# Moving three on-chip transposes of a recurrent attention kernel from TensorE to the DMA engines

## The chip, the cores and the metric

The kernel runs on one core of one Trainium2 chip. The metric is the device time of one execution in microseconds (us). The before and changed kernels were run in turn on the same chip. "PE" is TensorE, "PEld" its weight loads, "DVE" VectorE, "ACT" ScalarE, "POOL" GpSimd and "SP" the engine that issues the DMAs here.

## The reference, cut to what matters

Two identical layers follow each other. Each has an attention part A that walks over 64 segments of 32 rows and hands 8 memory rows from one segment to the next, and a gated feed-forward part B. Every part starts with a norm of its rows.

```
x = x + _A_ref(_layernorm(x), A_mem0, Wq, Wk, Wv, Wo, 32)   # layer 0
x = x + _B_ref(_layernorm(x), W_gate, W_up, W_down)
x = x + _A_ref(_layernorm(x), A_mem0, Wq, Wk, Wv, Wo, 32)   # layer 1, the same weights
x = x + _B_ref(_layernorm(x), W_gate, W_up, W_down)
# in _A_ref, for each segment s:
    h = concatenate([mem, xs])             # 8 + 32 rows of 448
    scores = q @ k^T / 16, masked;  p = softmax(scores);  o = (p @ v) @ Wo
    mem = o[:, :8];  outs.append(o[:, 8:])
```

## The kernel before: the parts that matter

The kernel runs layer 0 on segment t and layer 1 on segment t-4 in one step, 68 steps in all, two steps to a "pair" p of segments. Within a step the instructions go roughly: products of the keys with the folded query-key weights (hT,Mw, 224 matmuls), scores (TTm, TTs), softmax, P transposed (PTs), P @ h (PTs,hK), and for the memory rows the shorter chain PTm,hK, then Nw,UTm, then hi and lo, then selm,hi, whose result goes into the hT of the next step. Once a pair, the rest of the output projection (un), the norm of its rows (ln_b), the feed-forward part (b_layer) and the norm for the pair two later (ln_a).

Three blocks have to be transposed, because the products that read them take them with rows and columns exchanged: the rows of ln_a (xn into hT), the rows of ln_b (xn into xBT) and the probabilities (Ps into PTs). All three go through TensorE and are then copied out of PSUM:

```python
def ln_transpose(self, i, wr):
    T = S.tile("R", 1)
    S.mm(lambda: [MM(T.b().bitcast(BF)[:, c*128:c*128+128], S.xn[:, i, c*128:c*128+128], S.ident[:, :], is_transpose=True)
                  for c in range(4)], 4 * S.pitch(128), [("xn", i, 0), ("xn", i, 1), ("ident",)], T.res() + wr)
    return T
def ln_a(self, p):
    S.ln(S.XA[:, p % 4, :], ...)                       # row statistics, xn
    T = S.ln_transpose(0, [("hTx", pp, s) for s in range(2)])
    for s in range(2):
        S.cp(lambda s=s: S.hT[:, pp, s, :, :, 0:SEG], lambda s=s: ..., 256, T.res(), [("hTx", pp, s)])   # PSUM -> SBUF
    ...
def ln_b(self, p):                                     # the same, into xBT with one copy
def seg_pt(self, t):                                   # the same from Ps, into PTs with one copy
```

The order of instructions is not written by hand. The kernel lists operations with an estimated duration for each engine, and a list scheduler in it (class `_Order`) walks through a model of the engines and picks, at each free moment, the ready operation with the highest priority. A table `BIAS` adds a constant to the priority of each kind of operation.

## Time and profile before

| | before |
|---|---|
| time, median (range) of 4 runs | 1663.48 us (1662.29 to 1666.5) |
| span of the profiled run, granted PE clock | 1662.0 us, 0.994 |
| PE busy / idle | 1614.9 / 47.1 us |
| DVE, ACT busy | 1141.2, 717.2 us |

Idle is the span less the busy time. The first line of the page says the same; each entry is busy us, share of the span and number of instructions:

```profile
PE 1614.9 (97%) x30742; PEld 1192.9 (72%) x30742; DVE 1141.2 (69%) x3172; ACT 717.2 (43%) x2051; POOL 93.3 (6%) x156
```

PE is what bounds: it is busy for 97% of the span, and its groups show hardly any waiting. These are groups of PE instructions, each shape apart: line, operation, output and operands, shapes, count, then busy us and mean ns of one, then the idle time of PE just before the group and what ended it:

```profile
L127 PE MATMUL b<-hT,Mw 128*128 128x80 bf16 x13440 | 496.0, 202 | 0.7 <-ACT hT L696 0.7
L127 PE MATMUL b<-xBT,big 128*128 128x128 bf16 x3248 | 195.5, 219 | 0.4 <-DVE lo L913 0.4
L127 PE MATMUL b<-Nw,UTm 128*32 128x448 bf16 x3752 | 193.1, 357 | 2.1 <-DVE UTm L697 1.0 <-ACT UTm L696 0.6
L127 PE MATMUL b<-ident,xn 128*128 128x128 bf16 x276 | 27.7, 224 | 11.1 <-DVE xn L733 7.0 <-DVE seln L569 4.1
L127 PE MATMUL b<-ident,Ps 128*128 128x128 bf16 x272 | 26.7, 220 | 1.7 <-DVE Ps L859 1.7
L127 PE MATMUL b<-selm,hi 128*128 128x16 bf16 x268 | 22.0, 171 | 3.4 <-DVE lo L913 1.5
L127 PE MATMUL b<-PTs,hK 40*64 40x256 bf16 x256 | 20.6, 292 | 1.8 <-ACT big L696 0.5
```

The groups ident,xn and ident,Ps are the transposes. The busy time of these overlapping matmuls, 54.4 us, is not what they hold PE for: from start to next start, the two groups hold 40.2 us between 100 and 1655 us.

How close the hT hand-over is to its user can be read only from the timeline. This is the before kernel at the start of a pair; columns are start us, length us, engine, what, and in brackets the idle before it:

```profile
843.42 0.61 DVE L733 TENSOR_SCALAR xn<-XA,stat 128x448 bf16<-128x448 bf16 x2
844.08 0.40 PE L127 MATMUL b<-ident,xn 128*128 128x128 bf16 x4 [0.23 <-DVE xn L733]
844.52 0.49 DVE L697 COPY hT<-b 128x256 bf16<-128x256 bf16 x2 [0.49 <-PE b L127]
...
846.96 0.57 PE L127 MATMUL b<-Nw,big 128*64 128x448 bf16 x4
...
847.51 0.27 PE L127 MATMUL b<-hT,Mw 128*128 128x80 bf16 x3
```

The norm is done at 844.03, hT is complete at 845.01, and the segment that reads it starts at 847.51. So the hand-over took 1.0 us and had 2.5 us to spare. From the end of the norm to the start of its segment it is 3.48 us here and 4.98 us in the pairs between.

### The profile page before, as it was taken

The numbers are of one execution on the slowest core, as the hardware profiler recorded it, in microseconds if no ns is written. First come the engines' busy times: TensorE is split into PE (matmuls) and PEld (weight loads), VectorE is DVE, ScalarE is ACT, GpSimd is POOL, SyncE is SP. The second block draws the span as 40 slices with busy tenths as digits, with TensorE's granted clock in tenths as the row PEclk, the third lists the DMA queues.
The fourth block names the chain that finished last, engine by engine and source line by source line (L and its number), as shares of the span: only waits on it lengthen the run. The fifth ranks groups of instructions, "written<-read, shape, count | busy, mean of one in ns | idle before, by whom it ended". The sixth has DMA issues, their size and how long they took to land. (4 is left out here: it accounts for less than half of the span.)

```text
span 1662.0 us, 68199 instructions
## 1 busy us (share of the span) xinstructions
PE 1614.9 (97%) x30742; PEld 1192.9 (72%) x30742; DVE 1141.2 (69%) x3172; ACT 717.2 (43%) x2051; POOL 93.3 (6%) x156
## 2 busy tenths in 40 slices
PE   5999999999999999999999999999999999999998
PEld 2567777777776777777777777777677777766775
DVE  8757767666767767676776766676676767676665
ACT  4623443445343444544343444434334453433442
POOL 4000000000000000000000000000000000000000
PEclk8999999999999999999999999999999999999999
DMA  9710000000000000000000000000000000000000
GB/s 234 207 40 5 4 3 6 6 5 5 5 5 6 5 4 6 6 4 6 6 5 4 5 5 5 4 6 6 5 6 5 5 6 4 5 3 4 4 4 6
DMA packets 55762, 27.54 MB, mean 17 GB/s; under 512 B 44584, under 2 KB 54576, under 8 KB 55472
## 3 DMA queue, kind: packets, MB, share of 16 engines
q1 hardware_dynamic: 55120, 22.94, 5.7%
q8 instruction: 242, 3.96, 1.0%
q14 instruction: 48, 0.39, 0.1%
q10 hardware_dynamic: 352, 0.24, 0.1%
HBM read 10.33 MB, written 1.84 MB: 7 GB/s over the span
## 5 line engine op out<-in xcount | busy, mean ns | idle before, releaser
L127 PEld LDWEIGHTS b<-hT,Mw 128*128 128x128 bf16 x15232 | 535.2, 100 | 16.9 <-issue 8.6
L127 PE MATMUL b<-hT,Mw 128*128 128x80 bf16 (+1 forms) x15232 | 544.0, 199 | 3.2 <-issue 1.8
L127 PE MATMUL b<-Nw,big 128*64 128x448 bf16 (+1 forms) x1936 | 307.8, 355 | 0.6 <-DVE big L697 0.5
L697 DVE CAST TTs<-b 128x320 bf16<-128x320 f32 (+5 forms) x542 | 244.8, 454 | 13.2 <-PE b L127 12.5
L127 PE MATMUL b<-xBT,big 128*128 128x128 bf16 (+1 forms) x3920 | 217.1, 214 | 0.4 <-DVE lo L913 0.4
L127 PEld LDWEIGHTS b<-xBT,big 128*128 128x128 bf16 x3920 | 203.2, 98 | 7.2 <-ACT UTm L696 4.8
L127 PEld LDWEIGHTS b<-Nw,big 128*64 128x64 bf16 (+1 forms) x1936 | 128.8, 104 | 105.7 <-issue 14.0
L127 PE MATMUL b<-Nw,UTm 128*32 128x448 bf16 x3752 | 193.1, 357 | 2.1 <-DVE UTm L697 1.0
L696 ACT ACTIVATE TTm<-b 64x64 bf16<-64x64 f32 (+5 forms) x338 | 76.7, 227 | 266.7 <-PE b L127 262.7
L1053 DVE TENSOR_TENSOR hB<-gT,b 128x256 bf16<-128x256 bf16 x227 | 91.1, 412 | 119.4 <-ACT gT L1052 108.2
L127 PEld LDWEIGHTS b<-Nw,UTm 128*32 128x32 bf16 x3752 | 100.8, 97 | 88.7 <-issue 15.7
L697 POOL COPY hK<-xn 32x448 bf16<-32x448 bf16 x136 | 75.9, 558 | 1466.9 <-DVE xn L733 1460.4
L696 ACT ACTIVATE TTs<-b 64x256 bf16<-64x256 f32 (+4 forms) x342 | 141.4, 413 | 30.3 <-PE b L127 24.2
L697 DVE CAST TTm<-b 128x80 bf16<-128x80 f32 (+5 forms) x546 | 126.0, 233 | 38.9 <-PE b L127 10.2
L696 ACT ACTIVATE big<-b 128x512 bf16<-128x512 f32 (+1 forms) x242 | 124.5, 555 | 30.7 <-PE b L127 29.9
L697 DVE CAST UTm<-b 128x448 bf16<-128x448 f32 (+2 forms) x124 | 80.2, 647 | 81.0 <-PE b L127 80.1
L1052 ACT ACTIVATE gT<-b 128x256 bf16<-128x256 f32 x227 | 85.6, 380 | 90.7 <-PE b L127 73.0
L697 DVE CAST big<-b 128x512 bf16<-128x512 f32 (+1 forms) x146 | 85.4, 596 | 25.0 <-PE b L127 22.6
L127 PE MATMUL b<-big,hB 128*128 128x448 bf16 (+1 forms) x490 | 98.8, 354 | 0.0
L912 ACT ACTIVATE hi<-b 128x448 bf16<-128x448 f32 x67 | 36.5, 544 | 121.4 <-PE b L127 119.8
L127 PE MATMUL b<-PTs,hK 40*128 40x512 bf16 (+1 forms) x640 | 83.6, 346 | 4.8 <-ACT PTs L696 1.5
L696 ACT ACTIVATE UTm<-b 128x448 bf16<-128x448 f32 (+2 forms) x127 | 64.6, 523 | 24.4 <-PE b L127 23.3
(105 smaller groups left out, 1503.3 us busy)
## 6 DMA issues: line engine op xcount, KB each, us to landing
big<-in_A_Wo_dram SPq DMA_DIRECT2D x3, 896.0 KB, 5.8
out_dram<-ys SPq DMA_DIRECT2D x32, 56.0 KB, 1.9
big<-in_B_W_down_dram SPq DMA_DIRECT2D x1, 1568.0 KB, 7.1
XA<-in_A_x_dram SPq DMA_DIRECT2D x28, 56.0 KB, 2.2
big<-in_B_W_up_dram SPq DMA_DIRECT2D x1, 1344.0 KB, 5.9
big<-in_B_W_gate_dram SPq DMA_DIRECT2D x1, 1344.0 KB, 8.8
Nw<-in_A_Wo_dram SPq DMA_DIRECT2D x1, 896.0 KB, 6.4
XA<-in_A_x_dram ACTq DMA_DIRECT2D x4, 56.0 KB, 4.3
```

What stands on the lines that cost most here:

```text
L127: ins = E.matmul(out, lhsT=lhsT, rhs=rhs, **kw)
L696: return E.activation(out(), src(), ACT.Copy)
L697: return E.tensor_copy(out(), src())
L912: S.act(lambda E: E.activation(S.hi[:, :], C.b()[:, 0:D], ACT.Copy), D, C.res(), [("hi",)])
L1052: S.act(lambda E, k=k, R=R, n=n: E.activation(S.gT[:, k % 2, 0:n], R[0].b()[:, 0:n], ACT.Relu), n, R[0].res(), [("gT", k % 2)])
L1053: S.dve(lambda E, k=k, R=R, n=n, fcs=fcs: E.tensor_tensor(S.hB[:, fcs[0]:fcs[-1] + 1, 0:w], S.gT[:, k % 2, 0:n].rearrange("p (a b) -> p a ...
```

## The change

The intent: TensorE bounds, SP and the DMA engines are nearly idle after the weights are loaded (from 100 us on, the issues held SP for 28.7 us, and the DMA share was 0.02), so let the DMA engines transpose. The change gives each ln_a four transposes of 32x512, because the hT layout keeps 8 memory keys beside every 32 rows; its rows grow from 40 to 48 elements in it. The priorities were tuned anew.

```diff
+KROW = 48
 BIAS = {
-    "b_down": -5000.0, "b_layer": 2000.0, "ln_a": 41619.0, "p_t_mem": 500.0, "s_mem": 74990.0, ...
+    "b_down": -8324.0, "b_layer": -10663.0, "ln_a": -45000.0, "ln_b": 45000.0, "m_nat": -6708.0, ...
-        self.hT = self.sb("hT", [128, 2, 2, 4, 2, KEYS])
+        self.hT = self.sb("hT", [128, 2, 2, 4, 2, KROW])
     def ln_a(self, p):
-        T = S.ln_transpose(0, [("hTx", pp, s) for s in range(2)])
         for s in range(2):
-            S.cp(lambda s=s: S.hT[:, pp, s, :, :, 0:SEG], ..., 256, T.res(), [("hTx", pp, s)])
+            for l in range(2):
+                a = 64 * l + 32 * s
+                S.tdma(f"hT{s}{l}", lambda s=s, l=l: S.hT[:, pp, s, :, l, 0:SEG], lambda a=a: S.xn[a:a + 32, 0, :], 32,
+                       [("xn", 0, 0), ("xn", 0, 1)], [("hTx", pp, s, l)])
     def ln_b(self, p):
-        T = S.ln_transpose(1, [("xBT",)])
-        S.cp(lambda: S.xBT[:, :, :]..., 512, T.res(), [("xBT",)])
+        S.tdma("xBT", lambda: S.xBT[:, :, :], lambda: S.xn[:, 1, :], 128, [("xn", 1, 0), ("xn", 1, 1)], [("xBT",)])
+    def tdma(self, name, out, src, rows, rd, wr):
+        self.q.add("dma", ("sp",), {"sp": 60.0 + 4.0 * rows}, lambda E: E.dma_start_transpose(out=out(), in_=src()), rd, wr, name=name)
     def seg_pt(self, t):
-        (four transposes of Ps on TensorE and a copy of 512 columns)
+        S.tdma("pts", lambda: S.PTs[...], lambda: S.Ps[...], 128, [("Ps",)], [("PTs",)])
... (the readers of hT take 40 of its 48 elements; unchanged otherwise)
```

More of the change, by code (lines that the diff above doesn't have):

```diff
@@ L152 @@
 BIAS = {
-    "b_down": -5000.0, "b_layer": 2000.0, "ln_a": 41619.0, "p_t_mem": 500.0, "s_mem": 74990.0, "s_seg": 72560.0,
-    "seg_pt": -859.0, "u_mem": -38520.0, "u_seg": 2000.0, "un": -37811.0,
+    "b_down": -8324.0, "b_layer": -10663.0, "ln_a": -45000.0, "ln_b": 45000.0, "m_nat": -6708.0, "m_t": -3095.0,
+    "p_t_mem": 39621.0, "s_mem": 30914.0, "s_seg": 4852.0, "seg_pt": -500.0, "u_mem": -34712.0, "u_seg": -25197.0,
+    "un": -36918.0,
 }
@@ L289, in run @@
                 lim = max(f, t0) + (60.0 if e == "pe" else 40.0)
-                t, o = max((x for x in lst if x[0] <= lim), key=lambda x: (x[1].prio, -x[0]))
+                stay = BIAS.get("stay", 0.0) if e == "pe" else 0.0
+                t, o = max((x for x in lst if x[0] <= lim), key=lambda x: (x[1].prio + stay * (x[1].mode == mode), -x[0]))
                 if best is None or (t, -o.prio) < (best[0], -best[2].prio):
@@ L735, in ln @@
                   b - a, rd + [(key, 1), (key, 2)], [("xn", i, n)], 2)
-    def ln_transpose(self, i, wr):
-        S = self
-        T = S.tile("R", 1)
-        S.mm(lambda: [MM(T.b().bitcast(BF)[:, c * 128:c * 128 + 128], S.xn[:, i, c * 128:c * 128 + 128], S.ident[:, :], is_transpose=True)
-                      for c in range(4)], 4 * S.pitch(128), [("xn", i, 0), ("xn", i, 1), ("ident",)], T.res() + wr)
-        return T
     def ln_a(self, p):
@@ L747, in ln_a @@
         S.ln(S.XA[:, p % 4, :], [("XA", p % 4, 0), ("XA", p % 4, 1)], 0, "lnA", 0)
-        T = S.ln_transpose(0, [("hTx", pp, s) for s in range(2)])
         for s in range(2):
-            S.cp(lambda s=s: S.hT[:, pp, s, :, :, 0:SEG],
-                 lambda s=s: T.b().bitcast(BF)[:, 0:512].rearrange("p (c l s q) -> p c l s q", c=4, l=2, s=2)[:, :, :, s, :],
-                 256, T.res(), [("hTx", pp, s)])
+            for l in range(2):
+                a = 64 * l + 32 * s
+                S.tdma(f"hT{s}{l}", lambda s=s, l=l: S.hT[:, pp, s, :, l, 0:SEG], lambda a=a: S.xn[a:a + 32, 0, :], 32,
+                       [("xn", 0, 0), ("xn", 0, 1)], [("hTx", pp, s, l)])
         for s in range(2):
@@ L761, in ln_b @@
         S.ln(S.XB[:, p % 2, :], [("XB", p % 2, i) for i in range(3)], 16, "lnB", 1)
-        T = S.ln_transpose(1, [("xBT",)])
-        S.cp(lambda: S.xBT[:, :, :].rearrange("p a b -> p (a b)"), lambda: T.b().bitcast(BF)[:, 0:512], 512, T.res(), [("xBT",)])
+        S.tdma("xBT", lambda: S.xBT[:, :, :], lambda: S.xn[:, 1, :], 128, [("xn", 1, 0), ("xn", 1, 1)], [("xBT",)])
+    def tdma(self, name, out, src, rows, rd, wr):
+        self.q.add("dma", ("sp",), {"sp": 60.0 + 4.0 * rows}, lambda E: E.dma_start_transpose(out=out(), in_=src()), rd, wr, name=name)
     def t_unit(self, t, c, u0, m):
@@ L777, in mms @@
             return [MM(b[:, j * n:j * n + n], S.M[:, kt, 16 * c + u0 + j, :],
-                       S.hT[:, pp, s, kt, l0:l1, :].rearrange("p l x -> p (l x)"), start=(kt == 0), stop=(kt == 3))
+                       S.hT[:, pp, s, kt, l0:l1, 0:KEYS], start=(kt == 0), stop=(kt == 3))
                     for j in range(m) for kt in range(4)]
-        rd = [("hTx", pp, s)] + S.mkeys(pp, s, l0, l1)
+        rd = [("hTx", pp, s, l) for l in range(l0, l1)] + S.mkeys(pp, s, l0, l1)
         if t == 0:
@@ L806, in s_mem @@
         C = S.tile("R", 1)
-        S.mm(lambda: [MM(C.b()[:, l * KEYS:l * KEYS + KEYS], S.TTm[:, c, l, :], S.hT[:, pp, s, c, l, :], start=(c == 3), stop=(c == 2))
+        S.mm(lambda: [MM(C.b()[:, l * KEYS:l * KEYS + KEYS], S.TTm[:, c, l, :], S.hT[:, pp, s, c, l, 0:KEYS], start=(c == 3), stop=(c == 2))
                       for l in range(l0, l1) for c in (3, 0, 1, 2)], 100.0 * nl,
-             [("TTm",) + k for k in S.TKEYS] + [("hTx", pp, s)] + S.mkeys(pp, s, l0, l1), C.res())
+             [("TTm",) + k for k in S.TKEYS] + [("hTx", pp, s, l) for l in range(l0, l1)] + S.mkeys(pp, s, l0, l1), C.res())
         st = S.stat
@@ L835, in mms @@
                         out.append(MM(b[:, (qd * 2 + l) * KEYS:(qd * 2 + l) * KEYS + KEYS],
-                                      S.TTs[:, c, l, qd * 4:qd * 4 + 4, :].rearrange("p u q -> p (u q)"), S.hT[:, pp, s, c, l, :],
+                                      S.TTs[:, c, l, qd * 4:qd * 4 + 4, :].rearrange("p u q -> p (u q)"), S.hT[:, pp, s, c, l, 0:KEYS],
                                       start=False, stop=(l == l1 - 1 and qd == 3 and c == 2)))
@@ L862, in seg_pt @@
         S = self
-        G = S.tile("R", 1)
-        S.mm(lambda: [MM(G.b().bitcast(BF)[:, a * 128:a * 128 + 128], S.Ps[:, a, :], S.ident[:, :], is_transpose=True) for a in range(4)],
-             4 * S.pitch(128), [("Ps",), ("ident",)], G.res() + [("gseq",), ("PTs",)])
-        S.cp(lambda: S.PTs[:, :], lambda: G.b().bitcast(BF)[:, 0:512], 512, G.res(), [("PTs",)])
+        S.tdma("pts", lambda: S.PTs[:, :].rearrange("p (a x) -> p a x", a=4), lambda: S.Ps[:, :, :].rearrange("p a x -> p (a x)"), 128,
+               [("Ps",)], [("PTs",)])
     def p_t_mem(self, t):
```

## The prediction

> **What bounds it.** TensorE. The windows view has PE busy 1534.5 of the 1555 us from 100 to 1655, at clock 1.00; VectorE is busy 1063.8 and ScalarE 669.8 there. In the waits view the longest rows are other engines waiting for PE. So time goes out with PE start-to-start time and comes back with new PE waits.
>
> **What is removed.** 276 + 272 TensorE transposes (xn and Ps, by-form groups) in 137 groups of four. In the timeline of 800 to 893 us a group holds PE 0.22 us, or 0.33 us where it stands between products of another tiling (a switch costs about 0.10 us). From 100 to 1655 us that sums to 40.2 us; some switches stay, so I count 34 us. Also removed: the evictions PTs (597 ns x68), xBT (597 ns x35), hT (286 ns x62, some on ScalarE): about 80 us of engines that don't bound. The new order has about 7 fewer tiling switches per four segments.
>
> **What is added.** Per segment one 128x512 SBUF transpose by DMA for the probabilities, per pair four 32x512 and one 128x512 for the norms. Estimate of their latency from the weight transposes of this trace: 1024x448 holds the SP queue 3.7 us and lands about 2.2 us later; scaled by bytes a 128x512 takes 0.55 + 2.2 = 2.8 us, a 32x512 2.4 us. [...] no SBUF-to-SBUF transpose is in this trace. TensorE plus eviction took about 1.1 us, so each hand-over gets some 1.7 us longer. hT rows go from 40 to 48 elements, so the 80-column operand is in two pieces; I expect no cost, but 1 ns on each of 13440 matmuls would be 13 us.
>
> **On the critical path?** From the last scores to Ps took 2.9 to 3.2 us, so PTs is ready about 5.9 us after the scores. In the new order the PE work before the first product with PTs is, by measured starts, about 6.9, 9.4, 7.7 and 6.9 us in the four segments of a period: hidden, 1 to 3 us to spare. hT has two segments of slack: hidden. xBT after the odd-even product is the tight one: norm chain 3.5 to 4.1 us + 2.8 against about 6.1 us of work, so 0.5 to 1 us of wait, and the UTm product there has no filler after PTm, about 0.8 us. So per period (93.5 us) about 2.5 us out and 1.2 us back. Start: first hT and PTs transposes queue behind weight loads, +2 us. End: two bare norm transposes, +3 us.
>
> **Predicted:** 1640 us (-1.4%), 8 in 10 within 1620 to 1662. Faster over 2%: 0.27; within 2%: 0.63; slower: 0.10.
>
> **What would show it.** No ident,xn and ident,Ps groups; PE matmul count lower by 548; issue-to-landing of PTs and xBT 2.5 to 3.2 us in the DMA view; hT,Mw mean pitch still 35 to 37 ns; PE waits for DMA landings of xBT of 0.5 to 1 us about 17 times, hardly any for PTs and hT; VectorE and ScalarE together down about 80 us.
>
> **What would make it wrong.** SBUF-to-SBUF transposes landing after 4 us or more: then PTs waits appear in every segment and the change is even or slower. The split operand slowing PE. An SP instruction that waits ahead of a transpose in the in-order queue. Or an order that fills better than my budget: 1625.

What is cut from it, where marked, is a comparison of the two paths for a 128x128 block that no trace here shows. It was no term of the sum, which stays at about 2.5 us out and 1.2 us back in a period of 93.5 us. The 2 us at the start and 3 us at the end are estimates.

## More of the kernel before

The experiments ran later, on several chips, each batch with the kernel before beside it, whose medians there were 1662.75 to 1665.66 us; so differences of 2 or 3 us between batches are not read.

For a DMA the model takes a time on SP from the caller and 2200 ns until the data is there:

```python
LAT = {"pe": 170.0, "act": 0.0, "dve": 0.0, "pool": 60.0, "sp": 2200.0}
```

## The result, and the profile after

| | before | after |
|---|---|---|
| time, median (range) of 4 runs | 1663.48 us (1662.29 to 1666.5) | 1685.1 us (1680.17 to 1685.95) |
| span of the profiled run, granted PE clock | 1662.0 us, 0.994 | 1684.1 us, 0.990 |
| PE busy / idle | 1614.9 / 47.1 us | 1580.1 / 104.0 us |
| PE matmuls | 30742 | 30194 |

The change made the kernel 1.2% slower: ratio 1.0121, 95% interval 1.0097 to 1.0145. A ratio here is the mean time of one kernel's fast runs over that of the other's of the same rounds, so it is not quite the ratio of the medians quoted. The whole interval lies within 2%, but clear of 1.

The line of engines on the page after:

```profile
PE 1580.1 (94%) x30194; PEld 1168.1 (69%) x30194; DVE 1111.5 (66%) x3083; ACT 667.4 (40%) x1969; POOL 93.3 (6%) x156
```

PE is busy 34.8 us less, but waits 56.9 us more. The difference of the two is the 22.1 us by which the spans differ. The same groups of PE as before show where the waiting is:

```profile
L128 PE MATMUL b<-hT,Mw 128*128 128x80 bf16 x13440 | 494.6, 202 | 27.8 <-issue 20.9 <-DMA hT<-xn 5.7 <-DVE big L700 0.9
L128 PE MATMUL b<-xBT,big 128*128 128x128 bf16 x3248 | 215.9, 220 | 6.7 <-DMA xBT<-xn 6.7
L128 PE MATMUL b<-Nw,UTm 128*32 128x448 bf16 x3752 | 191.0, 355 | 15.1 <-DVE UTm L700 13.8 <-ACT UTm L699 1.3
L128 PE MATMUL b<-selm,hi 128*128 128x16 bf16 x268 | 21.5, 170 | 14.6 <-DVE lo L910 14.5
L128 PE MATMUL b<-PTs,hK 40*64 40x256 bf16 x256 | 20.5, 293 | 7.4 <-DVE big L700 6.7 <-DVE UTm L700 0.7
```

The largest is 27.8 us before hT,Mw, and the profile puts most of it down to "issue", which means that it found nothing the instruction waited for. The mean of one matmul is 202 ns as before, and since the ends of matmuls are modelled, the better sign is their pace: 224 in a row take 8.19 us in both kernels. The split operand cost nothing. The timeline at the start of a pair, against the one shown of before:

```profile
857.94 0.61 DVE L736 TENSOR_SCALAR xn<-XA,stat 128x448 bf16<-128x448 bf16 x2 [0.66 <-ACT stat L733]
858.57 5.00 SPq L762 DMA_TRANSPOSE hT<-xn  x4
...
860.02 0.95 PE L128 MATMUL b<-Nw,big 128*64 128x448 bf16 x8
...
862.22 0.48 PE L128 MATMUL b<-hT,Mw 128*128 128x80 bf16 x9 [1.25 <-issue]
```

Four transposes hold SP for 5.00 us. The segment starts 3.65 us after the first was issued. The first segment of a pair reads the first two of the four, one for each layer, and the trace's landing record of the second is 3.54 us after the first issue in nearly every pair; hT,Mw follows 0.09 us later. So the "issue" is a DMA landing that the profile did not match. In most pairs of the regular part PE waits there 1.25 us and 0.38 us in turn, so it was free to start the segment 2.4 and 3.3 us after the norm: about 1.1 and 1.7 us sooner than in the kernel before. The new order left less room for a hand-over that had become longer. The sizes of these DMAs come from the views of the tiles hT, xBT and PTs: the issue's time on SP in ns (least, median, most), and the us from issue to landing:

```profile
L762 SPq DMA_TRANSPOSE hT<-xn x136: 1161/1229/2308, 57.2 to 1633.1; - x136
DMA to landing us min/median/max: 2.3/2.3/5.9
L762 SPq DMA_TRANSPOSE xBT<-xn x35: 1189/1190/1680, 122.7 to 1672.4; - x35
DMA to landing us min/median/max: 2.4/2.4/2.8
L762 SPq DMA_TRANSPOSE PTs<-Ps x68: 1189/1191/2963, 75.9 to 1658.2; - x68
DMA to landing us min/median/max: 2.4/2.4/7.1
```

A 32x512 transpose holds SP for 1.23 us, as long as the 128x512 ones with four times the bytes. Two in a row therefore land at 1.23 + 2.3 = 3.5 us.

The second large wait is before Nw,UTm. It stands at one place in four segments:

```profile
875.13 0.49 PE L128 MATMUL b<-PTm,hK 40*128 40x128 bf16 x10
875.44 1.19 SPq L762 DMA_TRANSPOSE PTs<-Ps  x1
875.67 0.54 ACT L699 ACTIVATE UTm<-b 128x448 bf16<-128x448 f32 x1 [1.04 <-PE b L128]
875.87 0.61 DVE L700 CAST UTm<-b 128x448 bf16<-128x448 f32 x1
...
876.62 2.83 PE L128 MATMUL b<-Nw,UTm 128*32 128x448 bf16 x56 [1.00 <-DVE UTm L700]
```

Between PTm,hK and Nw,UTm only two evictions happen, and PE has nothing else that is ready. Before, the same gap was filled by the transposes of Ps and by products of un:

```profile
860.42 0.49 PE L127 MATMUL b<-PTm,hK 40*128 40x128 bf16 x10
860.84 0.40 PE L127 MATMUL b<-ident,Ps 128*128 128x128 bf16 x4
861.17 0.57 PE L127 MATMUL b<-Nw,big 128*64 128x448 bf16 x4
861.73 2.83 PE L127 MATMUL b<-Nw,UTm 128*32 128x448 bf16 x56
```

So there are two theories. Theory A: the hand-overs by DMA, above all hT with its serial issues, stand in front of products that have no work ahead of them to hide 2.4 to 3.5 us. Theory B: the new order, made by new priorities and a wrong table of costs, has used up the filler at other places, and the DMAs themselves have slack.

### The profile page after: what moved, and what is told of

Read it like the earlier page. It is cut to its first block, busy times and chain, and to the rows that moved or that the text cites. A ratio compares the mean times of both kernels' runs of the same rounds, so it can differ in the third digit from the quotient of the medians.

```text
span 1684.1 us, 67435 instructions
## 1 busy us (share of the span) xinstructions
PE 1580.1 (94%) x30194; PEld 1168.1 (69%) x30194; DVE 1111.5 (66%) x3083; ACT 667.4 (40%) x1969; POOL 93.3 (6%) x156
## 5 line engine op out<-in xcount | busy, mean ns | idle before, releaser
L128 PE MATMUL b<-Nw,big 128*64 128x448 bf16 (+1 forms) x1936 | 303.9, 357 | 1.5 <-ACT Nw L699 0.7
L128 PEld LDWEIGHTS b<-xBT,big 128*128 128x128 bf16 x3920 | 216.0, 98 | 43.0 <-DMA xBT<-xn 14.1
L128 PE MATMUL b<-xBT,big 128*128 128x128 bf16 (+1 forms) x3920 | 238.4, 215 | 7.6 <-DMA xBT<-xn 7.6
L128 PE MATMUL b<-Nw,UTm 128*32 128x448 bf16 x3752 | 191.0, 355 | 15.1 <-DVE UTm L700 13.8
L699 ACT ACTIVATE TTs<-b 128x320 bf16<-128x320 f32 (+4 forms) x338 | 139.1, 412 | 45.9 <-PE b L128 27.0
L699 ACT ACTIVATE big<-b 128x512 bf16<-128x512 f32 (+1 forms) x283 | 137.8, 543 | 10.1 <-PE b L128 9.5
L700 DVE CAST UTm<-b 128x448 bf16<-128x448 f32 (+2 forms) x108 | 69.6, 645 | 97.0 <-PE b L128 97.0
L128 PE MATMUL b<-big,hB 128*128 128x448 bf16 (+1 forms) x490 | 121.4, 355 | 0.3 <-DVE hB L1050 0.3
L699 ACT ACTIVATE UTm<-b 128x448 bf16<-128x448 f32 (+2 forms) x143 | 72.2, 528 | 93.7 <-PE b L128 93.2
L700 DVE CAST big<-b 128x512 bf16<-128x512 f32 (+1 forms) x105 | 66.9, 638 | 18.1 <-PE b L128 17.0
L128 PEld LDWEIGHTS b<-PTs,hK 40*128 40x128 bf16 (+1 forms) x640 | 22.9, 97 | 67.7 <-issue 26.3
```

The source lines that it names most:

```text
L128: ins = E.matmul(out, lhsT=lhsT, rhs=rhs, **kw)
L699: return E.activation(out(), src(), ACT.Copy)
L700: return E.tensor_copy(out(), src())
```

## The experiments

Each is a whole kernel. "Order kept" means that the streams of TensorE, VectorE and ScalarE are instruction for instruction those of the changed kernel; that was compared instruction by instruction. Ratios are to the kernel before, with its 95% interval.

| run | what | median us | ratio (interval) |
|---|---|---|---|
| e1_delay | order kept, one more transpose ahead of hT | 1744.19 | 1.0488 (1.0462 to 1.0514) |
| e2_skip | order kept, layer-0 transposes of hT left out | 1659.82 | 0.9975 (0.9955 to 0.9995) |
| e3_bias_old | changed kernel, priorities of before | 1735.59 | 1.0431 (1.0398 to 1.0464) |
| e4_before_bias_new | kernel before, new priorities | 1770.37 | 1.0644 (1.0627 to 1.0661) |
| e5_pool_copy | order kept, hT by one transpose and copies on POOL | 1671.34 | 1.0050 (1.0033 to 1.0066) |
| e6_before_tuned | kernel before, priorities searched | 1665.48 | 1.0014 (1.0001 to 1.0027) |
| e7_all_costed | changed kernel, measured costs, searched | 1679.39 | 1.0097 (1.0079 to 1.0114) |
| e8_hT_on_pe | as e7, hT on TensorE | 1660.01 | 0.9983 (0.9971 to 0.9996) |
| e9_pts_only | as e7, hT and xBT on TensorE | 1660.43 | 0.9984 (0.9971 to 0.9996) |
| e10_split | as e7, layer-0 half of the norm apart and early | 1676.24 | 1.0075 (1.0059 to 1.0090) |
| e11_copy_tuned | as e7, hT by one transpose and copies on VectorE | 1662.50 | 0.9993 (0.9978 to 1.0008) |
| e12_no_handover | order kept, all transposes left out | 1640.12 | 0.9852 (0.9835 to 0.9868) |

### A later and an earlier hT, with the order kept

e1_delay issues one more transpose just before the four:

```diff
+                if o.name == "hT00":
+                    self.sc.dma("hTd", <transpose xn[0:32] into a spare buffer>, res(o.rd), [("hTd",)], eng=o.fixed)
                 self.sc.dma(o.name, o.fn, res(o.rd), res(o.wr), eng=o.fixed)
```

> The changed kernel with its order of instructions kept, and one more 32x512 transpose by DMA (into a spare buffer) issued on SP just before the four of hT. Theory A (first segment of each pair waits for the landing of the second hT transpose, which the serial 1.24 us issues put 3.54 us after the first issue): that landing comes 1.24 us later, 33 pairs, so about +40 us on 1684, near 1724. Theory B (the loss is in the new order of PE work and its missing filler, hT has slack): no change, 1680 to 1688.

It went to 1744, 59 us up. The span of its profile is 1738.1, 54.0 up, and 38 us of that are waits before hT,Mw (29 to 67 us after the first 100 us), which is 33 pairs of about 1.2 us as expected. The pair shown above now reads:

```profile
887.36 1.16 SPq L500 DMA_TRANSPOSE hTd<-xn  x1
888.57 5.07 SPq L766 DMA_TRANSPOSE hT<-xn  x4
...
892.35 0.84 PE L128 MATMUL b<-hT,Mw 128*128 128x80 bf16 x19 [2.59 <-issue]
```

The wait of 1.25 us has become 2.59. The part that was not expected goes mostly with the granted PE clock, which fell from 0.990 to 0.984; that comes up again below.

e2_skip leaves out two of the four, so that the layer-1 transpose goes first:

```diff
+                if o.name in ("hT00", "hT10"):
+                    continue
```

> The changed kernel with its order kept, and the two layer-0 transposes of each hT set left out (those columns are zeroed once; the result is wrong on purpose). Theory A: the layer-1 transpose is then issued first and lands 1.28 us earlier; the waits before hT,Mw of 0.38 and 1.25 us in alternate pairs go, about -25 us, near 1659. Theory B: no change from 1684 beyond 5 us.

It ran in 1659.8, as theory A said (1659). The same group of the profile as above:

```profile
L128 PE MATMUL b<-hT,Mw 128*128 128x80 bf16 x13440 | 493.2, 202 | 3.8 <-DMA hT<-xn 2.5 <-DVE big L704 0.9
```

The two runs move the landing by one transpose in either direction, and the time follows: in this order hT has no slack, and the second serial issue alone costs 25 us. A caution: the output of this run is wrong, and yet the comparison with the reference passed. For this kernel a passed comparison says little about the attention part.

### The priorities

e3_bias_old and e4_before_bias_new swap the tables `BIAS` between the two kernels and change nothing else.

> The changed kernel with the priorities of the kernel before. Theory B (the new priorities order PE badly): 1640 to 1655, as PE busy stays 35 us under that of before and the waits fall to those of before. Theory A (latency of the hand-overs): 1680 or more, with the wait before hT,Mw still there.

> The kernel before with the priorities of the changed kernel. Theory B: 1680 to 1700, as the bad order comes with the priorities. Theory A: within 10 us of 1663.

Both got much slower, by 3% and 6% of their own kernels. So a table fits one code only. For e4 neither theory's number was met; for e3 theory A's "1680 or more" was, but not for its reason. With the old priorities the norm ends 4.2 and 5.2 us ahead of its segment in turn, and hT,Mw then waits 0.09 us or nothing for the same four transposes, which take 3.66 us; the loss is elsewhere (after the first 100 us, 48 us of waits before Nw,UTm and 30 us before PTs,hK). So the wait for hT needs both the longer hand-over and an order that leaves little room for it. What follows is a limit on method: when a part is put back in a kernel of this kind, the order must be kept, or the priorities searched again; the times of swapped tables say nothing about the change.

### A repair with the order kept

e5_pool_copy issues one 128x512 transpose, of the size of the other two, into a spare buffer, and lets the idle POOL spread it into hT. To make room, hT's rows go back to 40 elements and the output buffer is single instead of double.

```diff
-            four S.tdma(f"hT{s}{l}", ... 32 rows ...)
+            hTr <- transpose of xn[:, 0, :]                                       # one issue on SP
+            POOL: hT[:, pp, s, :, :, 0:SEG] <- hTr[...] for s in range(2)         # two copies of 128x256
```

> The changed kernel with the streams of TensorE, VectorE and ScalarE kept instruction by instruction; the four hT transposes of a pair are replaced by one 128x512 transpose into a spare buffer and two copies of 128x256 on the idle POOL, and the result is right. Theory A: the block lands 2.4 us after its issue as PTs and xBT do, a copy takes some 0.4 us, so hT is ready about 2.9 us after the issue for 3.63 before: 0.4 (all that is waited for) and 0.7 us out in alternate pairs, 33 pairs, -15 to -20 us on 1684: 1664 to 1670. Theory B (only order matters): 1680 to 1688.

```profile
848.47 1.19 SPq L759 DMA_TRANSPOSE hTr<-xn  x1
850.91 0.86 POOL L761 COPY hT<-hTr 128x256 bf16<-128x256 bf16 x2 [2.05 <-PE b L128]
851.36 8.20 PE L128 MATMUL b<-hT,Mw 128*128 128x80 bf16 x224 [0.50 <-POOL hT L761]
```

The time was 1671.3, 14 us under the changed kernel and 1 us slower than the range expected. hT is now ready 2.9 us after the issue (848.47 to 851.36) for 3.65. The waits before hT,Mw fell from 29 to 13 us, but those before xBT rose from 8 to 12 us: part of the gain was lost at the next hand-over.

### The same question with the order free

To compare at equal effort, the cost of a transpose in the scheduler's table was replaced by the measured one (1230 ns on SP, landing 2.3 to 2.4 us after the issue; it had 188 and 572 ns and 2200 more), and the priorities were searched against the kernel's own order model, with about 4800 trials for the control and about the same effort for the others. e6 is the control: the kernel before, searched likewise. e7 has all three by DMA, e8 puts hT back on TensorE, e9 xBT as well.

```diff
-        self.q.add("dma", ("sp",), {"sp": 60.0 + 4.0 * rows}, ..., name=name)
+        self.q.add("dma", ("sp",), {"sp": 1230.0}, ..., name=name, lat=1060.0 if rows < 128 else 1190.0)
```

> The control: the kernel before (all three transposes on TensorE), its priorities searched again by us against the kernel's own order model (about 4800 trials). The model's span falls 4 us from 1646 to 1642. If searching alone gives the gain: 1640 to 1655; if the old priorities were about as good as this search gets: 1657 to 1667.

> The changed kernel (all three transposes by DMA) with the measured cost put into its order model (1.23 us of SP for each transpose, landing 2.3 to 2.4 us after the issue) and its priorities searched again with the same effort. Theory A (the model took four hT transposes for 0.75 us of SP and so planned with hT that was not there): the waits before hT,Mw fall from 29 to under 10 us and the time to 1645 to 1662. If the latency of the hand-overs is the limit in any order: 1670 to 1690 again.

> As the run before, with the four hT transposes back on TensorE and PTs and xBT by DMA. Theory A: hT is the only hand-over without slack that costs more than it saves (10 us of PE for 29 us of waits), so this is 5 us or more under all three by DMA: 1638 to 1655.

> As the run before, with xBT on TensorE too: PTs alone by DMA, the one hand-over with 0.9 us or more of slack. Theory A: 20 us of PE out, under 10 us of waits back against before: 1640 to 1652, the fastest of the four. If slack of the hand-over does not matter: between before and all by DMA, 1663 to 1685.

The control stayed at 1665: searching alone gives nothing. e7 missed what theory A said of it and fell into the other range, 1670 to 1690. The waits before hT,Mw did fall, to 11 us, but others rose and the time stayed at 1679:

```profile
L128 PE MATMUL b<-hT,Mw 128*128 128x80 bf16 x13440 | 498.9, 203 | 11.0 <-issue 8.3 <-DVE big L696 0.5 <-DMA hT<-xn 0.4
L128 PE MATMUL b<-PTs,hK 40*128 40x512 bf16 x384 | 56.0, 380 | 6.5 <-DMA PTs<-Ps 6.5
L128 PE MATMUL b<-PTs,hK 40*64 40x256 bf16 x256 | 20.5, 293 | 20.2 <-DVE big L696 19.8 <-DVE UTm L696 0.4
```

So the wrong number in the table may explain much of the wait for hT, but not the loss, as far as one searched order can show: the order made with the right number pays elsewhere. Putting hT back on TensorE (e8) gave 19 us at once, more than the 5 us asked of it, but 1660.0 is 5 us above the range expected, 1638 to 1655. Putting xBT back too (e9) changed nothing more, and missed its range: PTs by DMA alone was expected to be the fastest at 1640 to 1652. Its profile has 1600.4 us of PE busy, 14.5 less than before, but 57.7 us idle for 47.1, 10.6 more, so its span is 1658.1 for 1662.0: nearly three quarters of the gain went to new waits.

### Two more ways to hand hT over by DMA

e10_split makes the norm of the layer-0 rows, which depend on nothing in the recurrence, a separate and early piece of work; only the layer-1 rows' transposes stay behind. e11_copy_tuned is the single transpose of e5 with two copies on VectorE in place of POOL. Both have the measured costs and searched priorities.

```diff
 def ln_a(self, p):
-    S.ln(S.XA[:, p % 4, :], ...)                 # one norm of 128 rows
+    for l in range(2):                           # e10: a norm of 64 rows for each layer, then its two transposes
+        <the same instructions on partitions 64*l to 64*l+64>
```

> A candidate that keeps all three transposes on DMA: the norm of the layer-0 rows and their two hT transposes, which need nothing of the recurrence, are separate and may go early, so only the layer-1 pair stands between the norm and the segment, the second of which no first segment waits for: landing 2.3 us after the issue for 3.54. Measured costs in the order model, priorities searched with about the effort of the run with all three by DMA. If the serial hT issues are what makes all by DMA slow (1679 with the same costs): 1645 to 1662, the waits before hT,Mw under 8 us. If any DMA in the loop costs about the same: 1670 to 1680.

> A second candidate, all three by DMA: one 128x512 transpose for hT into a spare buffer, then two copies on VectorE, priorities searched with about the same effort. Landing 2.4 us after the issue and two copies of about 0.2 us: hT ready some 0.8 us earlier than with four transposes. 1650 to 1668; under the 1671 of the POOL copies with the order kept, and not under the split one.

e10 missed its range and fell into the other one, 1670 to 1680. The hT landings hardly hold PE up any more, yet the time is 1676. A likely reason is that the extra norm instructions are on VectorE (busy 1158.0 us for 1111.5), which also makes lo for the memory rows:

```profile
L128 PE MATMUL b<-hT,Mw 128*128 128x80 bf16 x13440 | 496.6, 203 | 10.6 <-ACT hT L695 8.1 <-issue 1.2 <-DVE big L696 0.5
L128 PE MATMUL b<-selm,hi 128*128 128x16 bf16 x268 | 21.7, 170 | 22.7 <-DVE lo L918 22.7
```

That VectorE's added work is the cause of the 22.7 us is argued from this line, not tested; another order might do better. e11 came to 1662.5, inside its range and level with before, though it was not expected to come under e10: in this order all three transposes by DMA cost nothing overall, with one issue for hT in place of four. As e11 has another order than e7, the single issue as the cause rests on e5.

### What is left when no product waits for a transpose

> The changed kernel with the streams of TensorE, VectorE and ScalarE kept, and every transpose by DMA of hT, xBT and PTs left out (their buffers are zeroed once; wrong on purpose): no product waits for a transpose, its norm or its softmax any more. If the hand-overs by DMA make all of the loss: the waits of PE fall to those of the kernel before, about 20 us after the first 100, and the time to about 1630. If, beside them, the new order leaves PE without other work in the recurrence (before the UTm, selm and last PTs products, 14 + 13 + 9 us in the changed kernel): those waits stay at 30 to 36 us and the time is 1640 to 1650.

e12_no_handover leaves out all transposes of the changed kernel with the order kept (`continue` for hT00 to hT11, xBT and pts; the buffers are zeroed once; wrong). It takes the waits for the norms and softmaxes behind them away too.

```profile
L128 PE MATMUL b<-hT,Mw 128*128 128x80 bf16 x13440 | 491.7, 202 | 1.1 <-DVE big L709 0.9
...
L128 PE MATMUL b<-Nw,UTm 128*32 128x448 bf16 x3752 | 192.4, 357 | 15.1 <-DVE UTm L709 13.8 <-ACT UTm L708 1.3
L128 PE MATMUL b<-selm,hi 128*128 128x16 bf16 x268 | 21.5, 170 | 15.2 <-DVE lo L919 15.1
L128 PE MATMUL b<-PTs,hK 40*64 40x256 bf16 x256 | 20.6, 293 | 7.4 <-DVE big L709 6.7 <-DVE UTm L709 0.7
```

The time is 1640.1, and the waits before UTm, selm and the last PTs products are those of the changed kernel to within 0.6 us. So these 38 us are not waits for a transpose, as theory B has it; whether the priorities or merely the missing filler make them is not separated. The same three waits were 7.3 us already in the kernel before (2.1 + 3.4 + 1.8). Theory A holds for the rest, but with the norms and softmaxes ahead of the transposes in it. With the profiled spans the sum is:

| step | span us | PE busy | PE idle |
|---|---|---|---|
| before | 1662.0 | 1614.9 | 47.1 |
| new order, no transposes at all (e12) | 1638.2 (-23.8) | 1566.5 (-48.4) | 71.7 (+24.6) |
| and xBT, PTs and one hT ahead (e2) | 1658.5 (+20.3) | 1573.8 (+7.3) | 84.7 (+13.0) |
| and the second hT ahead (changed kernel) | 1684.1 (+25.6) | 1580.1 (+6.3) | 104.0 (+19.3) |

The work taken off PE was 48 us (43 us of it after the first 100 us, in which the weights are loaded). The order without transposes gave half of it back, mostly where PE had no other work in the recurrence of the memory rows (6 of the 24.6 us lie in the first 100 us); the hand-overs by DMA, norms and softmaxes included, gave back 46 us more.

### Waits followed by half clock

In the last two rows PE busy rises although the instructions are the same. The granted clock shows part of the reason. The windows view of the changed kernel around one long wait for hT; columns are the window, its length, busy us and counts of PE, PEld, DVE, ACT and POOL, the granted clock, DMA share and GB/s:

```profile
470.80:474.20 3.40, 1.16 (x23) 0.68 (x20) 1.03 (x2) 0.62 (x2) 0.47 (x1) 1.00 0.12 24
474.20:477.60 3.40, 3.40 (x56) 3.40 (x54) 1.45 (x4) 0.00 (x0) 0.00 (x0) 0.50 0.05 10
```

After a stretch of 3.4 us in which PE was busy for 1.16 us, it ran the next 3.4 us at half clock, with PE busy throughout. In e8 half clock came after a stretch with 2.03 us of PE busy:

```profile
578.80:582.20 3.40, 2.03 (x27) 0.79 (x24) 3.16 (x7) 2.96 (x9) 0.00 (x0) 1.00 0.19 39
582.20:585.60 3.40, 3.40 (x46) 3.40 (x45) 1.67 (x3) 1.31 (x4) 0.00 (x0) 0.51 0.00 0
```

In the clock records of the traces before and after, every stretch below full clock is at 0.50, and each but the last of a trace is 3.41 us long or two or three times that. What sets them off was not shown: after 2.00 us of PE busy in the changed kernel (1440.2 to 1443.6) the next 3.4 us ran at full clock. The mean granted clocks were 0.994 before, 0.990 after, 0.984 in e1 and 0.995 in e12. In the first two, the stretches at half clock sum to 20.5 and 32.3 us of the span. As an estimate from these, 10 and 16 us of clock were not granted, so about 6 of the 22 us are this.

## Why the prediction was wrong

What held:

- PE bounds, and the work taken off it: 34 us of transposes and 7 tiling switches for every four segments were predicted, about 2.5 us per period; e12, where half-clock stretches blur it least (mean clock 0.995), has 43 us less PE busy after the first 100 us, 2.5 us in each of 17 periods. That PE busy of the changed kernel fell by 34.8 us, so near the 34, is chance. The matmul count fell by 548, as said. DVE and ACT together fell by 79.5 us (80 predicted).
- The landing of a single transpose: 2.8 us predicted for 128x512 and 2.4 measured, 2.4 predicted for 32x512 and 2.3 measured.
- PTs is hidden: its landing stands 0.9 to 3.9 us ahead of the first use in the regular part, and PE waited 1.6 us in all for it in the changed kernel.
- xBT and UTm: waits of 0.5 to 1 us and 0.8 us at one place in a period were predicted, and 6.7 us in 16 waits (most of 0.34 us, so less than predicted) and 13.8 us in 16 (most of 1.0 us) were measured.
- The split operand costs nothing (224 matmuls in 8.19 us before and after).

What failed:

- The step that failed is "hT has two segments of slack: hidden." hT had 2.5 us of slack before, not two segments, and less in the new order, where PE was free 2.4 and 3.3 us after the norm and the hand-over took 3.66 us. The layer-1 half of its rows comes out of b_layer of the pair two earlier, and that is finished only just before the segment that reads it. The changed kernel waits 27.8 us there. e1 (a landing 1.2 us later, +59 us), e2 (one issue less ahead, -25 us) and e5 (one issue for four, -14 us) show it as cause.
- Beside it stands a size that made it worse: the time of a transpose on SP was scaled by bytes from weight transposes of 1024x448 (3.7 us), which gives 0.13 us for a 32x512. It measured 1.23 us, as much as for 128x512 (1.19). The second of two in a row so lands after 3.5 us and not 2.5. The kernel's scheduler had a cost as small in its table (188 ns, then 2200 to the landing), which fits the room of 2.4 us that its order left. With the measured cost (e7) the waits for hT fell from 29 to 11 us.
- The sum "about 2.5 us out and 1.2 us back" per period therefore had its second term too small: 56.9 us of new waiting in 17 periods is 3.3 us each. hT is 27 us of it; waits for lo before selm, which were not in the budget at all, are 11 us (14.6 for 3.4).
- None of the reasons listed for being wrong explains the loss: the transposes landed fast (2.3 to 2.4 us in the median, single ones up to 7.1), the operand was free (8.19 us for 224 matmuls in both kernels), and what held up the SP queue ahead of hT was the transposes themselves (5.00 us for four, one after the other), not an instruction that waited.

What stays open: how much of the order's own waits (UTm, selm, the last PTs) another order could fill. Our search left all versions with hT by four DMAs at 1676 to 1679 and those with a quicker hT at 1660 to 1663, with one order tried on the chip for each, so differences of 3 us between them are not to be read. The two fastest kernels that leave nothing out, e8 and e9, are 0.2% under the kernel before and 1.5% under the changed one.

## What to carry to other kernels

Before moving work off the engine that bounds, find for each hand-over how long its user waits after it today. The latency of 2 to 4 us here was nearly free only where that slack was larger (PTs landed 0.9 to 3.9 us ahead of its use and cost 1.6 us of waits; hT took 3.66 us where there was room for 2.4 and 3.3, and cost 27.8), and in a recurrence slack must be read from the timeline, not from the order of the program. Count what a small DMA costs its issuing queue (1.2 us here), and make one issue of several where a chain waits for all of them (14 us less in e5). In this kernel the engine that bounds, 97% busy with work from a recurrence, had little filler left, so taking work off it turned part of the gain into waits, and some of the clustered waits were followed by half clock (3.4 us at 0.50 after 3.4 us with 1.16 us of PE busy).
